# Moving four small on-chip transfers to later places in the sync queue of an attention and spectral-mix kernel

## Chip, cores and metric

The kernel runs on one core of a Trainium2 chip. The metric is device time in microseconds (us), the median of several executions. The trace has its own clock, which starts at the first instruction; its span is 1.7 to 2.6 us shorter than the measured time.

## The reference

Two steps, in float32: causal attention in a sliding window of 64 positions, then a mix in frequency space with a residual, a channel product and a rectification.

```python
x = attention(q, k, v)                      # 8 batches, 8 heads, 576 positions, 64 wide
X = np.fft.rfft(x, axis=1)                  # first 64 modes only
Yr = einsum(Xr, w_r) - einsum(Xi, w_i)      # one 512 x 512 complex matrix per mode
Yi = einsum(Xr, w_i) + einsum(Xi, w_r)
u = x + irfft(Y)                            # 8 x 576 x 512
out = u + maximum(u @ w_ch, 0)
```

## The kernel before

Most of the time goes into streaming the weights of the 64 modes. The change lies in the last 34 us, the **output stage**. By then the spectrum of each batch lies in a tile of 128 rows, of which only the last eight are missing: they belong to the last four modes, whose weights come last. One product brings these rows of all batches into one tile, `yl`. For each of batches 2 to 7, eight rows are carried from there to partitions 120 to 127 by a transfer from one on-chip tile to another, 32 KB each:

```python
def send(b):
    r0 = 2 * R + RL * (b - 2)               # RL = 8
    nc.sync.dma_start(out=batch_tile(b)[128 - RL:].bitcast(FP32), in_=yl[r0:r0 + RL].bitcast(FP32))
```

Then 36 row tiles of 128 x 512 are made. PE transforms the spectrum back (`add`), ACT rectifies, PE adds the rest, DVE adds the residual (`finish`), and the sync queue (SP) writes the result, two tiles in one transfer of 512 KB. A fifth, half-length tile of a batch pair goes out as two transfers of 64 rows.

```python
def finish(n):
    b, t = seq[n]
    add(n, "Yb", True)
    ...
    nc.vector.tensor_tensor(out=ot[:, j], in0=ps, in1=x_sb[:, b, t, :], op=ALU.add)
    if t == NT - 1:
        for i, queue in enumerate((nc.sync, nc.sync)):                  # L885
            queue.dma_start(out=out[b + i, 128 * t:, :], in_=ot[64 * i:64 * i + 64, 0])
    elif j:
        nc.sync.dma_start(out=out[b, ...], in_=ot)                      # L890, 512 KB

for n in range(NT):
    rectify(n)                                                          # add(n, "yw"), then Relu on ACT
    if n == 2:
        nc.scalar.copy(out=yl[0:NR, 0], in_=psw[0:NR])
send(2)
turn_of = {1: 3, 3: 4, 5: 5, 7: 6, 8: 7}     # after row tile n, the rows of this batch
for n in range(NQ):
    finish(n)
    if n in turn_of:
        send(turn_of[n])
    ...                                      # rectify(n + 3): up to three tiles ahead
```

So rows and outputs share one queue, which takes its instructions in order.

The softmax here doesn't subtract the row's maximum and nothing guards it: scores larger than these inputs give would overflow.

Of the kernel before, what the change touches and what calls it, by code (L numbers as in the profile page):

```python
# [20 lines left out]
def view(ap, off, dims):  # L21

    return bass.AP(ap.tensor, ap.offset + off, [list(ap.ap[0])] + [list(d) for d in dims])
# [3 lines left out]
def kernel(  # L27
# [662 lines left out]
    def batch_tile(b):  # L690

        if b not in Yp:
            Yp[b] = wmid.tile([128, 2, DM], FP32R, name=f"Y{b}", tag=f"wm{b}")
        return Yp[b]

    def pair_tile(what, b):

        return batch_tile(b)[:, ("yw", "Yb").index(what), :]

    def parts_of(b, t):  # L700
        return [(b, 0, 128)] if t < NT - 1 else [(b, 0, 64), (b + 1, 64, 64)]
# [5 lines left out]
    def turned(lhs, m, psa, psw):  # L707
        for e in range(NC):
            nc.tensor.matmul(out=psw[:m, :], lhsT=lhs(e), rhs=wch[:, e, :], start=(e == 0), stop=(e == NC - 1))  # L709
        for e in range(NC):  # L710
            nc.tensor.transpose(out=psa[:m, e, :], in_=lhs(e), identity=ident_r)
# [34 lines left out]
    def on_act(n):  # L746
        return n >= len(PLACES) and (seq[n][1] == NT - 1 or n in (11, 16, 19, 25, 30, 33))

    def lay(n):
        ps = tps[n] = bank([128, DM], FP32, "pso8")  # L750
        if on_act(n):
            nc.scalar.copy(out=ps, in_=channel_out(tiles.index(seq[n])))
            return
        nc.tensor.matmul(out=ps, lhsT=ident_r, rhs=channel_out(tiles.index(seq[n])), start=True, stop=False,
                         skip_group_check=True)
# [78 lines left out]
    with tc.manual_schedule(engines={mybir.EngineType.PE, mybir.EngineType.Activation, mybir.EngineType.DVE,  # L834
                                     mybir.EngineType.Pool, mybir.EngineType.SP}):
        nc.vector.tensor_copy(out=view(YT2, R - RL, [[NR, NC], [R, 2], [1, RL]]),
                              in_=view(psl, 0, [[RL * B, NC], [RL, 2], [1, RL]]))
        nc.vector.tensor_copy(out=YT2[:, :, 2 * R:], in_=psl[:, :, 2 * RL:])
        psa = ps_a.tile([128, NC, 128], FP32R, name="psa", tag="psa")
        psw = ps_a.tile([128, DM], FP32, name="psw", tag="psw")  # L840
        turned(lambda e: YT2[:, e, 0:NR], NR, psa, psw)
        lay(EARLY_ROWS)
        flat = psa.rearrange("p c e -> p (c e)")
        yl = yp.tile([128, 2, DM], FP32R, name="yl")

        def send(b):
            r0 = 2 * R + RL * (b - 2)
            nc.sync.dma_start(out=batch_tile(b)[128 - RL:].bitcast(FP32), in_=yl[r0:r0 + RL].bitcast(FP32))

        for b in range(2):  # L850
            nc.scalar.copy(out=pair_tile("yw", b)[E0:], in_=psw[R * b:R * b + R])
            nc.vector.tensor_copy(out=pair_tile("Yb", b)[E0:], in_=flat[R * b:R * b + R])
        nc.vector.tensor_copy(out=yl[0:NR, 1], in_=flat[0:NR])

        def add(n, what, stop):
            b, t = seq[n]
            for bb, r0, k in parts_of(b, t):
                tr = 128 * t + (64 - r0 if t == NT - 1 else 0)
                nc.tensor.matmul(out=tps[n], lhsT=trigI[:, tr:tr + 128], rhs=pair_tile(what, bb),  # L859
                                 start=False, stop=stop and r0 + k == 128, skip_group_check=True)  # L860

        def rectify(n):
            add(n, "yw", True)
            nc.scalar.activation(out=tps[n], in_=tps[n], func=ACT_F.Relu)  # L864

        ots = {}
# [4 lines that stand above are left out]
            if t % 2 == 0:  # L871
                ots[0] = op.tile([128, 2, DM], FP32, name="ot")
            ot, j = ots[0], t % 2
            ps = tps.pop(n)
            if n == NQ - 1:
                to = out[b, 128 * t - 128:128 * t + 128, :].rearrange("(p j) e -> p j e", j=2)
                for c0, queue in ((0, nc.sync), (DM // 2, nc.scalar)):
                    cc = slice(c0, c0 + DM // 2)
                    nc.vector.tensor_tensor(out=ot[:, 1, cc], in0=ps[:, cc], in1=x_sb[:, b, t, cc], op=ALU.add)
                    queue.dma_start(out=to[:, 1, cc], in_=ot[:, 1, cc])  # L880
                return
# [4 lines that stand above are left out]
            elif n == NQ - 2:  # L886
                nc.sync.dma_start(out=out[b, 128 * t:128 * t + 256, :].rearrange("(p j) e -> p j e", j=2)[:, 0],
                                  in_=ot[:, 0])
            elif j:
                nc.sync.dma_start(out=out[b, 128 * t - 128:128 * t + 128, :].rearrange("(p j) e -> p j e", j=2),  # L890
                                  in_=ot)

        AHEAD = 3
        for n in range(NT):
            rectify(n)
            if n == 2:
                nc.scalar.copy(out=yl[0:NR, 0], in_=psw[0:NR])
        send(2)
        turn_of = {1: 3, 3: 4, 5: 5, 7: 6, 8: 7}
        for n in range(NQ):  # L900
            finish(n)
            if n in turn_of:
                send(turn_of[n])
            nxt = n + AHEAD + 2
            new = nxt if n and EARLY_ROWS < nxt < NQ else None
            if new and on_act(new):
                lay(new)
            for r in {2: [5]}.get(n, [n + AHEAD] if AHEAD <= n < NQ - AHEAD else []):
                rectify(r)
            if new and not on_act(new):  # L910
                lay(new)
# [30 lines left out]
```

## Time and profile before

| | before |
|---|---|
| time, median of the first 3 runs | 429.73 us (429.59 to 430.24) |
| span of the trace | 427.3 us (its run took 429.12 us) |
| output stage, from ACT's first copy of the last rows (393.70) to the end of the span | 33.64 us |
| end of the last DVE instruction | 420.39 us |
| last packet of output ends | 426.1 us |

Three more lines of the windows view are needed for the comparison later (columns: stretch, its length, busy time and count of PE, PEld, DVE, ACT and POOL, PE clock, DMA share, GB/s).

```profile
410.00:413.00 3.00, 3.00 (x15) 2.41 (x14) 2.90 (x5) 3.00 (x7) 0.00 (x0) 1.00 0.98 358
416.00:419.00 3.00, 3.00 (x12) 1.76 (x10) 3.00 (x6) 2.55 (x6) 0.00 (x0) 1.00 1.00 370
419.00:422.00 3.00, 0.10 (x1) 0.00 (x0) 1.39 (x4) 0.00 (x0) 0.00 (x0) 1.00 1.00 372
```

The DMA share says how much of the 16 engines' time is covered by packets, GB/s how much they moved. The two must be read together: a packet that is held up counts as busy. In this trace packets of 4 KB lasted 0.159 us at the median and up to 1.03 us.

### The profile page before, as it was taken

What the parts mean: (1) busy time and instruction counts of PE and PEld (TensorE: products, weight loads), DVE (VectorE), ACT (ScalarE), POOL (GpSimd) and SP (SyncE); (2) the same over time, 40 slices, a digit from 0 to 9 for tenths busy, and PEclk for the clock granted to TensorE, in tenths of its full rate; (3) what the DMA queues carried; (4) which work ended last, traced back from release to release, by engine and by line L of the source; (5) the groups of instructions that cost most, each with busy time, mean ns of one, the idle gap of its engine ahead of it and who ended that gap; (6) DMA issues with size and microseconds to landing.
All of it is one profiled execution on the core that took longest, in us unless ns stands there. A gap on an engine that the chain in (4) does not pass through costs nothing.

```text
span 427.3 us, 11629 instructions
## 1 busy us (share of the span) xinstructions
PE 322.1 (75%) x5179; PEld 230.8 (54%) x5186; DVE 176.1 (41%) x372; ACT 164.1 (38%) x290; POOL 89.4 (21%) x171
## 2 busy tenths in 40 slices
PE   6989998998998866422488877876367685498992
PEld 5755765765665566411367666654245452266781
DVE  5566765765764200306223332221113332141993
ACT  4585765866863221001022322222012221131991
POOL 7231231241112232211221221221111122100000
PEclk9999998999996655555588998899556965589997
DMA  7999999999999999999999999999999999993698
GB/s 142 212 213 213 213 212 213 214 211 214 214 213 213 214 213 261 214 214 213 213 213 215 213 212 214 214 214 213 212 215 213 214 213 214 214 214 68 219 351 333
DMA packets 28721, 92.16 MB, mean 216 GB/s; under 512 B 2896, under 2 KB 3152, under 8 KB 28672
## 3 DMA queue, kind: packets, MB, share of 16 engines
q0 software_dynamic: 25344, 81.80, 96.1%
q1 hardware_dynamic: 3184, 9.50, 6.0%
q8 instruction: 40, 0.66, 0.6%
q10 hardware_dynamic: 144, 0.13, 0.1%
q14 instruction: 9, 0.07, 0.0%
HBM read 162.53 MB, written 9.44 MB: 402 GB/s over the span
## 4 chain that ended last, share of the span: by engine, by line
DMA 51%; PE 32%; DVE 8%; issue 4%; ACT 2%; POOL 1%; DVEq 0%; POOLq 0%
DMA wt<-in_moe_w_i_dram 45%; PE pso L316 7%; PE pst L218 6%; DMA wy<-in_moe_w_i_dram 4%; PE pso L859 4%; PE psv L235 3%; DVE x_sb L324 3%; PE pss L372 3%; PE pss L272 2%; DMA wt<-in_moe_w_r_dram 2%; PE psx L338 2%; PE pss L291 2%; DVE vT L59 2%; PE psw L709 1%; DVE ot L882 1%
## 5 line engine op out<-in xcount | busy, mean ns | idle before, releaser
L563 PE MATMUL psy<-XQ,wt 128*128 128x16 bf16 x1616 | 61.4, 191 | 72.8 <-DMA wt<-in_moe_w_i_dram 37.6
L563 PEld LDWEIGHTS <-wt 128*128 128x128 bf16 x1616 | 53.2, 103 | 87.5 <-DMA wt<-in_moe_w_i_dram 42.4
L591 DVE CAST xT<-pxt 128x256 fp32r<-128x256 bf16 (+1 forms) x68 | 26.1, 434 | 61.8 <-PE pxt L584 39.4
L115 POOL DMA_DIRECT2D wt<-in_moe_w_r_dram x54 | 29.0, 537 | 87.8 <-DMA wt<-in_moe_w_r_dram 42.2
L596 ACT CAST Z<-psz 128x512 fp32r<-128x512 f32 x36 | 21.1, 586 | 66.9 <-PE psz L594 66.6
L115 POOL DMA_DIRECT2D wt<-in_moe_w_i_dram x52 | 27.9, 536 | 84.7 <-DMA wt<-in_moe_w_i_dram 53.7
L594 PE MATMUL psz<-wch,xT 128*128 128x512 f32 x144 | 45.3, 457 | 0.0
L297 ACT ACTIVATE et<-pss 128x512 bf16<-128x512 f32 x72 | 39.2, 599 | 13.2 <-PE pss L291 13.2
L316 PE MATMUL pso<-vt,et 128*64 128x65 bf16 (+1 forms) x576 | 34.3, 210 | 5.2 <-DVE x_sb L324 5.1
L316 PEld LDWEIGHTS <-et 128*64 128x64 bf16 (+1 forms) x576 | 23.9, 114 | 17.3 <-issue 9.8
L594 PEld LDWEIGHTS psz<-wch,xT 128*128 128x128 f32 x144 | 29.2, 217 | 5.8 <-ACT Z L596 0.4
L324 DVE TENSOR_TENSOR x_sb<-pso,rcp 128x640 bf16<-128x640 f32 x32 | 26.3, 822 | 0.9
L859 PE MATMUL pso<-Y,trigI 128*128 128x512 f32 x80 | 23.1, 402 | 0.1
L59 DVE CAST YT<-psy 128x256 fp32r<-128x256 f32 x6 | 2.5, 423 | 49.4 <-PE psy L563 49.4
L882 DVE TENSOR_TENSOR ot<-pso,x_sb 128x512 f32<-128x512 f32 x35 | 22.2, 685 | 1.5 <-PE pso L859 1.1
L59 DVE CAST x_sb<-psj 128x512 bf16<-128x512 f32 x16 | 11.0, 688 | 27.2 <-PE psj L771 27.1
L58 ACT CAST YT<-psy 128x256 fp32r<-128x256 f32 x6 | 2.2, 373 | 50.7 <-DVE YT L59 50.7
L272 PE MATMUL pss<-band,ident_bf 64*64 64x512 bf16 x136 | 20.5, 414 | 1.5 <-ACT et L297 1.5
L59 DVE COPY vT<-pst 128x768 bf16<-128x768 bf16 x16 | 15.3, 957 | 13.0 <-PE pst L218 13.0
L58 ACT CAST x_sb<-psj 128x512 bf16<-128x512 f32 x16 | 9.4, 586 | 26.9 <-PE psj L771 26.9
L864 ACT ACTIVATE pso<-pso 128x512 f32<-128x512 f32 x36 | 19.1, 597 | 0.0
L859 PEld LDWEIGHTS pso<-Y,trigI 128*128 128x128 f32 x80 | 14.5, 188 | 5.5 <-ACT pso L864 1.7
(158 smaller groups left out, 496.3 us busy)
## 6 DMA issues: line engine op xcount, KB each, us to landing
wt<-in_moe_w_r_dram POOLq DMA_DIRECT2D x54, 512.0 KB, 19.1
wt<-in_moe_w_i_dram POOLq DMA_DIRECT2D x52, 512.0 KB, 19.1
out_dram<-ot SPq DMA_DIRECT2D x15, 512.0 KB, 4.2
rk<-in_k_dram POOLq DMA_DIRECT2D x8, 576.0 KB, 9.0
rq<-in_q_dram POOLq DMA_DIRECT2D x8, 576.0 KB, 12.9
rv<-in_v_dram POOLq DMA_DIRECT2D x8, 576.0 KB, 11.9
wy<-in_moe_w_r_dram POOLq DMA_DIRECT2D x3, 512.0 KB, 16.9
wy<-in_moe_w_i_dram POOLq DMA_DIRECT2D x3, 512.0 KB, 19.1
```

The costliest lines, as they stand in the source:

```text
L59: return nc.vector.tensor_copy(out=o, in_=i)
L115: nc.gpsimd.dma_start(out=wt, in_=src[m].rearrange("(p c) e -> p c e", c=NC))
L218: nc.tensor.transpose(out=ps[64 * hh:64 * hh + 64, c, :], in_=src[:, hh, (c0 + c) * D:(c0 + c + 1) * D], identity=ident_bf)
L272: nc.tensor.matmul(out=pss[(2 * w + hh) % 3][64 * half:64 * half + 64, :], lhsT=ident_bf[pp, pp], rhs=view(band[pp], 128 * half, [[0, WIN ...
L297: nc.scalar.activation(out=et[:, hh, :], in_=pss[(2 * w + hh) % 3], func=ACT_F.Exp, scale=EX_SCALE)
L316: nc.tensor.matmul(out=pso[po, hh, (i // 2) * VW:(i // 2) * VW + D + 1], lhsT=et[pk, hh, col:col + 64], rhs=vt[pk, 1 - f % 2, 2 * hh + g / ...
L324: nc.vector.tensor_tensor(out=view(x_sb, b * NT * DM + g * D, [[4 * D, 2], [DM, NT], [1, D]]), in0=view(pso, 0, [[512, 2], [VW, NT], [1, D]]),
L563: nc.tensor.matmul(out=psy[:, m % MG, e, :], lhsT=w[:, c, 128 * e:128 * e + 128], rhs=XQ[:, c, :, 1 - im:3 - im, m], start=(m % MG == im + ...
L591: nc.vector.tensor_copy(out=xT[:, :, w * k:w * k + w], in_=view(psts[k], j, [[128, NC], [n, w]]))
L594: nc.tensor.matmul(out=psz, lhsT=xT[:, c, :], rhs=wch[:, c, :], start=(c == 0), stop=(c == NC - 1))
L859: nc.tensor.matmul(out=tps[n], lhsT=trigI[:, tr:tr + 128], rhs=pair_tile(what, bb), start=False, stop=stop and r0 + k == 128, skip_group_c ...
L882: nc.vector.tensor_tensor(out=ot[:, j], in0=ps, in1=x_sb[:, b, t, :], op=ALU.add)
```

## The change

Batch 2 and batch 3 stay where they were. The rows of batches 4 to 7 move to later places, so that the first outputs are not held up behind transfers that nobody needs yet. Each still leaves eight or more tiles ahead of its first use.

```diff
-        turn_of = {1: 3, 3: 4, 5: 5, 7: 6, 8: 7}
+        turn_of = {1: 3, 5: 4, 9: 5, 12: 6, 15: 7}
         for n in range(NQ):
             finish(n)
             if n in turn_of:
                 send(turn_of[n])
```

## The prediction

> **What bounds the kernel now.** I began with the page. Its utilisation rows cut the span into 40 slices of 10.7 us.
>
> ```profile
> span 427.3 us, 11629 instructions
> ...
> PE   6989998998998866422488877876367685498992
> ...
> DMA  7999999999999999999999999999999999993698
> GB/s 142 212 213 213 213 212 213 214 211 214 214 213 213 214 213 261 214 214 213 213 213 215 213 212 214 214 214 213 212 215 213 214 213 214 214 214 68 219 351 333
> ```
>
> Up to about 391 us the DMA engines bring in weights at nines. The change touches nothing there. It acts in the last three and a half slices, where the row of DMA reads 3, 6, 9, 8: the output stage. It starts when PE begins the inverse transform at 394.3 us, and 36 row tiles pass through PE, ACT, DVE and the sync queue. So the second view is the chain of waits in order of time, and its last piece matters.
>
> ```profile
> 420.06 0.33 DVE ot L879
> ```
>
> All arithmetic is done at 420.4 us, yet the span is 427.3 us. For the last 7 us only data already computed is travelling. The chain calls the stage PE and DVE; the last instruction it can name is DVE's, so I checked the transfers myself, with the windows view (columns: busy time and count of PE, PEld, DVE, ACT, POOL, then PE clock, DMA share, GB/s).
>
> ```profile
> 399.00:401.00 2.00, 2.00 (x10) 1.60 (x9) 1.71 (x4) 2.00 (x6) 0.00 (x0) 1.00 0.98 320
> 401.00:403.00 2.00, 2.00 (x10) 1.52 (x10) 1.91 (x5) 2.00 (x6) 0.00 (x0) 1.00 0.89 340
> 403.00:405.00 2.00, 2.00 (x11) 1.61 (x10) 1.80 (x3) 2.00 (x6) 0.00 (x0) 1.00 0.94 375
> 405.00:407.50 2.50, 2.50 (x12) 2.05 (x11) 2.40 (x5) 2.50 (x6) 0.00 (x0) 1.00 0.70 216
> 407.50:410.00 2.50, 2.50 (x12) 2.01 (x11) 2.30 (x5) 2.50 (x6) 0.00 (x0) 1.00 1.01 398
> 413.00:416.00 3.00, 3.00 (x15) 2.42 (x14) 2.68 (x5) 2.98 (x7) 0.00 (x0) 1.00 1.03 407
> 422.00:425.50 3.50, 0.00 (x0) 0.00 (x0) 0.00 (x0) 0.00 (x0) 0.00 (x0) 0.50 1.01 391
> ```
>
> From 407.5 to 425.5 us the 16 DMA engines are full (share 1.0). The stage is bound by the writing of 9.4 MB of output. Before 407.5 us there is one hole: 0.70 between 405.0 and 407.5. Every microsecond lost there appears at the end, because nothing behind it has slack to recover it. The timeline of the sync queue shows who made the hole (start, length, line; L848 is the last rows' transfer, L890 an output of two tiles, L885 the two half outputs of a last row tile).
>
> ```profile
> 401.52 0.65 SPq L848 DMA_DIRECT2D Y<-yl  x1
> 402.22 0.88 SPq L890 DMA_DIRECT2D out_dram<-ot  x1
> 403.26 0.65 SPq L848 DMA_DIRECT2D Y<-yl  x1
> 404.02 1.42 SPq L885 DMA_DIRECT2D out_dram<-ot  x2
> 405.55 0.68 SPq L848 DMA_DIRECT2D Y<-yl  x1
> 406.33 0.85 SPq L890 DMA_DIRECT2D out_dram<-ot  x2
> 407.27 2.16 SPq L885 DMA_DIRECT2D out_dram<-ot  x2
> ```
>
> Between the 512 KB output issued at 402.22 and the next one at 406.33 lie 4.1 us with two small transfers of last rows and only 256 KB of output. One 512 KB output keeps the engines busy for about 1.27 us (128 packets at a median of 0.159 us, over 16 engines), the pair of L885 for about 0.7. So about 2 us of work stood against 4.1 us: the queue ran dry. DVE was not late: the tiles of the output issued at 406.33 were ready at 403.6, those of the following one at 405.1. The sync queue, issuing small transfers, was.
>
> **What the Trainium skill says.** The page "Perfetto Trace Analysis", section "What "DMA-bound" means", names as one case the DMA sequencer whose track is solid DMA slices, that time being descriptor generation. The trace agrees for 402 to 407 us only; later the engines themselves are full. The same page, section "DMA Instruction — HWDGE (DVE, Sync)", says that the profiled window of such an issue does not contain the data's movement. The trace agrees: the output issued at 397.94 first moves many packets at about 399.0, and the one at 406.33 at about 407.3, so an issue feeds the engines 1.0 us later. "DMA: Bandwidth & Descriptors", section "Why a DMA increments its semaphore by 16 and not by 1", says a transfer issued this way uses the largest number of engines up to 16 that divides its slowest dimension; eight rows therefore use 8. The trace agrees: each of these six transfers moves eight packets of 4096 bytes. The same page, section "Issuing engines are not separate DMA queues", says all issuers share the same 16 engines; so the small transfers always take some DMA time, wherever they stand.
>
> **The change part by part.** Nothing is added or removed: six transfers of 32 KB before and after, the same instructions in the same order on PE, DVE, ACT and POOL. Only SP's order differs. The rows of batch 4 leave after row tile 5 instead of 3, batch 5 after 9 instead of 5, batch 6 after 12 instead of 7, batch 7 after 15 instead of 8. Each costs the sync queue 0.65 to 0.68 us plus 0.1 for the semaphores ahead of it.
>
> I lay SP's list anew with these durations, 0.5 us for an output not held up, and no issue before DVE's result:
> - Output 5 (named by its last tile) goes at 400.2 instead of 400.85, output 7 at 401.7 (its tile is ready at 401.62) instead of 402.22.
> - The halves of tile 8 go at 402.5 and 403.2 instead of 404.02 and 404.85.
> - Batch 5's rows at 403.95; output 10 at 404.65 instead of 406.33; output 12 at 405.15 instead of 406.80.
> - Batch 6's rows at 405.7, the halves of tile 13 from 406.4 instead of 407.27, output 15 at 408.0 to 408.7 instead of 409.52, batch 7's rows next.
>
> Now the engines, 1.0 us behind. Work that arrives from 399.0: outputs 1, 3, 5, 7 are 5.1 us, tile 8 0.7, three small transfers about 0.15 to 0.4 each. The engines have work until about 405.7, and output 10 arrives at 405.7. So the 2.5 us hole closes almost wholly: (1 - 0.70) x 2.5 = 0.75 us won. From 401 to 405 the loss is 0.11 x 2 + 0.06 x 2 = 0.34 us, and I count a third of it, 0.1. Against this I leave 0.1 us for what remains at the seam. Sum: 0.75 + 0.1 - 0.1 = **0.75 us** less. After 407.5 SP has room for the two late transfers: 16.5 us pass up to its last issue, but unhindered issues there would need about 10 (seven of L890 at 0.5, six of L885 at 0.65, plus gaps, an estimate). The last results stay at 420.4 us; the last two issues are now 1.7 and 2.5 us behind DVE, so pulling them 0.75 us forward is possible.
>
> **The rivals.**
> - **The late rows make PE wait.** Batch 7 is first read by PE at 412.4 us. Its transfer now starts at 408.4 to 409.3, behind three outputs. In the kernel before these transfers landed 2.4 to 3.6 us after issue, outputs in the full stretch 3.5 to 5.0. That gives 410.8 to 412.9, at worst over 413: PE could wait up to about 1 us. For it: the queue is fuller there. Against it reaching the end: the DMA backlog is some 4 us deep then and the outputs concerned are issued 1.3 to 2.5 us after DVE. It would cost at most 0.3 us, giving 429.3.
> - **The small transfers cost more in a full queue.** Eight packets around 400.5 us took about 0.9 us each instead of 0.16, half of the engines, which is about 0.4 us of the 16; later ones took about 0.3 us per packet. If each of the three moved transfers cost 0.4, the gain would be gone: 429.9. I hold this for unlikely, since the four later ones were cheap.
> - **The hole is hidden anyway**, if PE and DVE set the end: then 429.7. Against it: 7 us of transfers after the last DVE instruction.
> - **More is won**: all of 405 to 407.5 and 401 to 405, which is 1.1 us: 428.6.
>
> **Range and chances.** 429.73 - 0.75 = 428.98, rounded to 428.95 us. Below it, the largest win and a little noise give 428.3; above it, the rival of dear transfers gives 429.9. The three runs of before spread over 0.65 us, which is nearly the effect itself. Two per cent would be 8.6 us, and the whole stage's idle DMA time is about 1.1 us: within 2% at 0.98.
>
> **What would show it.** Right: the DMA share between 405 and 407.5 rises from 0.70 to over 0.9; the second output after tile 8 is issued before 405.5 instead of 406.80; DVE still ends within 0.3 us of 420.4; the last SP issue and the span end about 0.75 us earlier. Wrong: a wait of PE's loads at L859 for the DMA of the last rows near 409 or 412 us together with a later DVE end; or an unchanged end in spite of a filled hole, with low GB/s at a share of 1.0 where the small transfers now lie, which would mean the transfers' own cost was moved and not the issue time.

## The result

| | before | changed |
|---|---|---|
| median | 429.81 us (429.59 to 430.24, 4 runs) | 429.67 us (429.39 to 430.07, 4 runs) |
| ratio | | 0.9996, 95% interval 0.9979 to 1.0014 |
| output stage in the trace | 33.64 us | 33.70 us |

Ratios are the mean time of one kernel's runs over that of the other's in the same rounds, so not quite the ratio of the medians. No difference between the two kernels can be told from the noise. A later set of five runs says the same (`after_again`: 1.0005, interval 0.9991 to 1.0018). The profiled run of the changed kernel was the slowest of its four, 430.07 us, and that of the kernel before, 429.12 us, was faster than all four of its timed runs above. The changed kernel's output stage began 0.47 us later; so I compare the stages from their own beginnings. There is only one trace of the kernel before, so how far its own stage varies is not known.

The page of the changed kernel, its span, and its rows for DMA:

```profile
span 427.9 us, 11629 instructions
...
DMA  7999999999999999999999999999999999993698
GB/s 143 212 212 213 213 214 213 213 212 212 215 212 209 214 214 259 215 213 214 213 213 214 213 214 214 213 214 214 214 213 213 213 214 214 213 213 62 228 349 325
```

Slices of 10 us show nothing: the digits are the same. The windows view, with the stretches of before moved by 0.47 us, shows more:

```profile
401.47:403.47 2.00, 2.00 (x10) 1.53 (x9) 1.91 (x5) 2.00 (x6) 0.00 (x0) 1.00 0.92 360
403.47:405.47 2.00, 2.00 (x11) 1.60 (x10) 1.80 (x3) 2.00 (x5) 0.00 (x0) 1.00 1.01 369
405.47:407.97 2.50, 2.50 (x12) 2.04 (x11) 2.40 (x5) 2.50 (x6) 0.00 (x0) 1.00 0.86 318
407.97:410.47 2.50, 2.50 (x12) 2.01 (x11) 2.29 (x5) 2.50 (x6) 0.00 (x0) 1.00 0.95 337
410.47:413.47 3.00, 2.58 (x12) 1.74 (x10) 2.90 (x5) 2.92 (x6) 0.00 (x0) 1.00 0.97 357
416.47:419.47 3.00, 3.00 (x14) 2.15 (x12) 2.99 (x6) 3.00 (x7) 0.00 (x0) 1.00 0.95 350
419.47:422.47 3.00, 0.87 (x2) 0.25 (x2) 2.17 (x5) 0.32 (x1) 0.00 (x0) 1.00 0.99 344
```

Read the last column against the lines of before. In the stretch of the hole the changed kernel moves 318 GB/s in place of 216: (318 - 216) x 2.5 us = 255 KB more. In the very next stretch it moves 337 in place of 398, (398 - 337) x 2.5 = 152 KB less. The two late stretches give back (370 - 350) x 3 = 60 and (372 - 344) x 3 = 84 KB. In these traces the gain is there, and it is handed back before the end. Summed over all packets of the output queues, rows included, from the stage's beginning, the changed kernel is ahead of the kernel before by:

| us after the stage's beginning | 13.8 | 16.3 | 19.3 | 22.3 | 25.3 | 28.3 |
|---|---|---|---|---|---|---|
| changed, KB ahead | 289 | 145 | 130 | 101 | 46 | -49 |
| changed, second trace | 297 | 140 | 92 | 49 | 31 | -79 |

At about 410 GB/s, the highest rate of a stretch, 289 KB are 0.70 us: what the prediction promised, at the place where it promised it.

Not every column can be taken as it stands. The half outputs go in packets of 2 KB, which took longer for their bytes: 0.107 us on average in the changed kernel, against 0.171 us for packets of twice the size. At 16.3 us the changed kernel has 222 of these packets behind it and the kernel before 143, so a part of the drop there is only their order. At 13.8, 19.3, 25.3 and 28.3 us the counts are equal, to two packets. Read from those columns, more than half of the lead is gone 5.5 us after the hole, and all of it at 28.3 us.

What follows the hole is in the timeline of the sync queue of the changed kernel (start, length, line):

```profile
403.16 1.82 SPq L885 DMA_DIRECT2D out_dram<-ot  x2
405.09 0.68 SPq L848 DMA_DIRECT2D Y<-yl  x1
405.87 0.85 SPq L890 DMA_DIRECT2D out_dram<-ot  x2
406.89 0.69 SPq L848 DMA_DIRECT2D Y<-yl  x1
407.67 1.83 SPq L885 DMA_DIRECT2D out_dram<-ot  x2
409.59 0.53 SPq L890 DMA_DIRECT2D out_dram<-ot  x1
410.23 0.69 SPq L848 DMA_DIRECT2D Y<-yl  x1
```

There are three of the four moved transfers (the first, of batch 4, went at 401.08), each followed by outputs that come 0.7 us later for it. And there is something else: the pair at 403.16 took 1.82 us for its two issues, where before it took 1.42. The queue is not free to issue whenever it wants.

The waits show a second cost, first the kernel before, then the changed one (waiting engine and line, what it waited for: total us, times, longest):

```profile
DVE ot L882 <- PE pso L859: 1.1, 5, 0.3
```

```profile
DVE ot L882 <- PE pso L859: 1.9, 5, 1.0
PEld pso L859 <- DMA Y<-yl: 0.9, 1, 0.9
```

PE's weight load waits 0.9 us for the rows of batch 7, which were issued at 410.23 and had landed at 413.5. DVE loses 0.8 us by it. The chain of waits ends with the same instruction as before, 0.78 us later from the stage's beginning (27.47 against 26.69 us):

```profile
421.30 0.33 DVE ot L879
```

### The profile page after: what moved, and what is told of

The parts are those of the page before. It is cut to its first block, busy times and chain, and to the rows that moved or that the text cites. A ratio compares the mean times of both kernels' runs of the same rounds, so it can differ in the third digit from the quotient of the medians.

```text
span 427.9 us, 11629 instructions
## 1 busy us (share of the span) xinstructions
PE 324.8 (76%) x5179; PEld 232.9 (54%) x5186; DVE 176.8 (41%) x372; ACT 164.1 (38%) x290; POOL 89.2 (21%) x171
## 4 chain that ended last, share of the span: by engine, by line
DMA 54%; PE 30%; DVE 8%; issue 3%; ACT 2%; POOL 1%; DVEq 0%; POOLq 0%; SPq 0%
DMA wt<-in_moe_w_i_dram 41%; DMA wy<-in_moe_w_r_dram 9%; PE pso L316 7%; PE pst L218 6%; PE psv L235 3%; DMA wt<-in_moe_w_r_dram 3%; DVE x_sb L324 3%; PE pss L372 3%; PE pso L859 2%; PE pss L272 2%; DVE ot L882 2%; PE psx L338 2%; PE pss L291 2%; DVE vT L59 2%; ACT vt L58 1%
## 5 line engine op out<-in xcount | busy, mean ns | idle before, releaser
L594 PE MATMUL psz<-wch,xT 128*128 128x512 f32 x144 | 47.6, 475 | 0.0
L594 PEld LDWEIGHTS psz<-wch,xT 128*128 128x128 f32 x144 | 30.8, 229 | 6.2 <-ACT Z L596 0.3
L58 ACT CAST x_sb<-psj 128x512 bf16<-128x512 f32 x16 | 9.4, 585 | 25.3 <-PE psj L771 25.3
```

The source lines that it names most:

```text
L594: nc.tensor.matmul(out=psz, lhsT=xT[:, c, :], rhs=wch[:, c, :], start=(c == 0), stop=(c == NC - 1))
```

## The experiments

Two theories stood at the start. **Theory A**: the gain is eaten by PE's wait for late rows. **Theory B**: the hole in the DMA's work only moved. For the second set a third was put on record, **theory C**: each small transfer holds up the eight engines that it uses, these finish every later output late, and the sync queue is held by them. That set's results suggested another form, which I use below: the small transfers take DMA time of their own, which cost nothing while it lay in the hole. In the expectations, "1.4 us" and "2.0 us" of PE's wait are the wait of the weight load and that of the matmul added up; they lie partly beside each other, so the real waits are 0.9 and 1.2 us.

For each trace I also summed the durations of all packets of the output queues, divided by 16 (**DMA work**), and took what is left between the tenth large packet and the last one (**DMA idle**). Packets overlap a little, so these sums are good to perhaps 0.2 or 0.3 us, and two traces of the same changed kernel differ by 0.57 us in the stage.

| run | median us | before | ratio (95% interval) | stage us | DMA work us | DMA idle us |
|---|---|---|---|---|---|---|
| before | | | | 33.64 | 26.00 | 0.93 |
| changed | 429.67 | 429.81 | 0.9996 (0.9979 to 1.0014) | 33.70 | 26.29 | 0.70 |
| after_again | 430.32 | 430.07 | 1.0005 (0.9991 to 1.0018) | 34.27 | 26.39 | 1.14 |
| b7_early | 429.92 | 429.58 | 0.9995 (0.9971 to 1.0019) | 33.89 | 26.25 | 0.94 |
| b7_later | 430.15 | 429.58 | 1.0003 (0.9980 to 1.0027) | 34.35 | 26.45 | 1.20 |
| pool_sends | 429.92 | 429.58 | 1.0000 (0.9975 to 1.0024) | 34.30 | 26.64 | 1.11 |
| halves | 432.82 | 429.58 | 1.0071 (1.0048 to 1.0095) | 36.81 | 26.16 | 3.71 |
| tiny_before | 429.91 | 429.81 | 0.9995 (0.9983 to 1.0007) | 33.75 | 25.12 | 1.83 |
| tiny_after | 429.26 | 429.81 | 0.9988 (0.9975 to 1.0001) | 32.90 | 25.14 | 0.94 |
| pool_rest | 429.88 | 429.81 | 1.0019 (0.9987 to 1.0052) | 32.93 | 25.98 | 0.14 |
| no_sends | 428.18 | 429.81 | 0.9969 (0.9954 to 0.9984) | 32.08 | 24.88 | 0.95 |
| copy_early | 429.85 | 430.07 | 0.9996 (0.9983 to 1.0008) | 33.57 | 26.31 | 1.01 |
| pool_paced | 429.88 | 430.07 | 0.9989 (0.9977 to 1.0002) | 33.66 | 26.67 | 0.49 |
| halves_spread | 432.56 | 429.94 | 1.0062 (1.0044 to 1.0079) | 36.67 | 26.24 | 3.29 |

### b7_early: the last two batches land in time

```diff
-        turn_of = {1: 3, 5: 4, 9: 5, 12: 6, 15: 7}     (changed kernel)
+        turn_of = {1: 3, 5: 4, 9: 5, 10: 6, 12: 7}
```

> The changed kernel, but batch 6's rows leave after row tile 10 and batch 7's after 12 (instead of 12 and 15), so that they land before PE needs them near 412.9 us. Theory A (PE's wait of 1.4 us for batch 7's rows ate the gain): the wait is gone, DVE ends about 1 us earlier than in the changed kernel, and the time is 428.9 to 429.2 us. Theory B (the sync queue's own outputs hold it up and the hole in the DMA only moved): the wait is gone too, but the time stays within 0.2 us of 429.7, and the DMA's idle time between its first and last output packet stays near 1.4 us.

PE no longer waits for rows, and DVE ends at 26.66 us of the stage, as in the kernel before. The time did not move. Theory A alone is out: the gain stays away without the wait too. The windows, aligned to the stage again, show where it goes:

```profile
405.19:407.69 2.50, 2.50 (x12) 2.04 (x11) 2.40 (x5) 2.50 (x6) 0.00 (x0) 1.00 0.86 319
407.69:410.19 2.50, 2.50 (x12) 2.02 (x11) 2.30 (x5) 2.50 (x6) 0.00 (x0) 1.00 0.84 290
```

Both late transfers now stand in the second stretch, and it falls to 290 GB/s (398 in the kernel before). The lead drops from 297 KB to 38 KB at once. The hole moved, as theory B said.

### b7_later: the last batch still later

```diff
-        turn_of = {1: 3, 5: 4, 9: 5, 12: 6, 15: 7}     (changed kernel)
+        turn_of = {1: 3, 5: 4, 9: 5, 12: 6, 18: 7}
```

> The changed kernel, but batch 7's rows leave only after row tile 18 instead of 15, so about 2 to 3 us later: PE must wait for them some 3 to 4 us instead of 1.4. Theory A (such a wait passes on to the end): 431 to 432.5 us, with a hole in the DMA after 416 us. Theory B (the backlog of the DMA, some 4 us, swallows it): at most 430.3 us.

```profile
DVE ot L882 <- PE pso L859: 4.8, 7, 2.3
ACT pso L864 <- PE pso L859: 3.1, 2, 2.0
PEld pso L859 <- DMA Y<-yl: 2.2, 1, 2.2
```

DVE ends 2.85 us later in the stage than in the changed kernel (30.32 against 27.47). The stage is 0.65 us longer than in the first trace of the changed kernel and 0.08 us longer than in the second; the time is within the noise. The backlog of the DMA swallows nearly all of a wait of this length, as theory B expected and theory A did not.

### pool_sends: the sync queue issues outputs only

```diff
-            nc.sync.dma_start(out=batch_tile(b)[128 - RL:].bitcast(FP32), in_=yl[r0:r0 + RL].bitcast(FP32))
+            nc.gpsimd.dma_start(out=batch_tile(b)[128 - RL:].bitcast(FP32), in_=yl[r0:r0 + RL].bitcast(FP32))
```

> The kernel before, with all six transfers of last rows issued by the otherwise idle POOL engine, so that the sync queue issues outputs only and all rows land by about 405 us. If the small transfers' issue time on the sync queue made the hole (Theory A, and the prediction): no wait of PE, outputs after row tile 8 issued near 404 and 405.2 us, hole closed, 428.6 to 429.0 us. Theory B (the sync queue is held up by its own outputs): the time stays within 0.3 us of 429.8, with single issues of 1 us and more already before 405 us.

The first output starts 0.8 us earlier, and still there is no gain. All six transfers now go at once, batch 2's rows come too late, and PE's load waits:

```profile
PEld pso L859 <- DMA Y<-yl: 1.2, 1, 1.2
```

In this trace the next output is issued only at 402.80 us, 2.5 us after the one before it. Later, one issue of a half output takes 1.72 us, from 414.04 on, and 0.3 to 0.6 us after its end only two to four packets are under way at a time, where 16 are usual. The landing records fit a queue that was held while engines that had run ahead ran dry: of the output issued at 412.44, 15 engines had finished within 0.55 us, one came 1.38 us after the first. That is a reading, in the sense of theory B. The single issues of 1 us and more before 405 us that theory B had named did not come; the longest took 0.85. And the run mixes two causes, so it settles less than I wanted.

### halves: twice as many small transfers, the same bytes

```diff
-            nc.sync.dma_start(out=batch_tile(b)[128 - RL:].bitcast(FP32), in_=yl[r0:r0 + RL].bitcast(FP32))
+            for i in range(2):
+                nc.sync.dma_start(out=batch_tile(b)[128 - RL:, i].bitcast(FP32),
+                                  in_=yl[r0:r0 + RL, i].bitcast(FP32))
```

> The kernel before, with each transfer of last rows cut into two of half the bytes: twelve issues instead of six, the same bytes, so 6 x 0.7 us more of the sync queue's time between 397 and 406 us. If the issue time of these transfers decides how full the DMA is (the prediction): the hole before 407.5 us grows by 2 to 3.5 us and the time is 431.5 to 433.5 us. If it is hidden behind the sync queue's other waits (Theory B): under 430.5 us.

As the prediction's mechanism said: six more issues of 0.62 to 0.68 us, and 3.2 us more at the end. DMA work stays at 26.2 us, DMA idle grows from 0.93 to 3.71. Its windows (this trace's stage begins 2.1 us later than before's):

```profile
405.00:410.00 5.00, 5.00 (x23) 4.06 (x22) 4.68 (x9) 5.00 (x12) 0.00 (x0) 1.00 0.70 250
410.00:413.00 3.00, 3.00 (x15) 2.40 (x14) 2.80 (x5) 3.00 (x8) 0.00 (x0) 1.00 0.60 163
```

So the issue time of small transfers does reach the end of the kernel. This part of the prediction's reasoning holds.

### tiny_before and tiny_after: the same issues, hardly any bytes

Both give a wrong result: each transfer carries 64 bytes of each of its eight rows. (The comparison with the reference did not flag it; it is wrong by construction all the same.) Nothing else differs from the kernel before and the changed kernel.

```diff
-            nc.sync.dma_start(out=batch_tile(b)[128 - RL:].bitcast(FP32), in_=yl[r0:r0 + RL].bitcast(FP32))
+            nc.sync.dma_start(out=batch_tile(b)[128 - RL:, 0, 0:16].bitcast(FP32),
+                              in_=yl[r0:r0 + RL, 0, 0:16].bitcast(FP32))
```

> Wrong result on purpose: the kernel before, with the six transfers of last rows in the same places, but each carrying only 64 bytes of each of its eight rows (0.5 KB instead of 32 KB). The sync queue still issues all six; the DMA engines hardly work for them. Theory of the issue time (the prediction): the hole at 405 to 407.5 us stays and the time is within 0.2 us of the kernel before, the output stage 33.4 to 33.7 us long. Theory C (each transfer holds up the eight engines it uses by 0.5 to 1 us, those eight then finish every later output late, and the sync queue is held by the slow ones): the landings of one output stay within 0.5 us of each other, and the time is 0.5 to 1 us below the kernel before.

> Wrong result on purpose: the changed kernel, with its transfers of last rows in their later places but carrying only 64 bytes per row. Against the run with small transfers in the old places this shows what the new places are worth when the transfers cost no DMA time. Theory of the issue time: 0.7 to 0.9 us below the kernel before, since the hole closes and the rows land soon enough that PE waits little. Theory C: at least as far below the kernel before as the other one, 1 to 1.5 us, with no split of landings in two halves of eight after 411 us.

The stretch of the hole in the old places, then in the new ones (the stages of both traces begin at 393.73 us, as good as in the kernel before):

```profile
405.00:407.50 2.50, 2.50 (x12) 2.04 (x11) 2.40 (x5) 2.50 (x7) 0.00 (x0) 1.00 0.76 230
```

```profile
405.00:407.50 2.50, 2.50 (x12) 2.02 (x11) 2.39 (x5) 2.50 (x7) 0.00 (x0) 1.00 0.88 347
```

With the issues kept and the bytes gone, the time did not fall by the 0.5 to 1 us that theory C had named for `tiny_before`. The four kernels make a square:

| stage us / DMA work / DMA idle | old places | new places |
|---|---|---|
| 32 KB | 33.64 / 26.00 / 0.93 | 33.70 / 26.29 / 0.70 (second trace 34.27 / 26.39 / 1.14) |
| 0.5 KB | 33.75 / 25.12 / 1.83 | 32.90 / 25.14 / 0.94 |

Go down the left column: the bytes are taken away, the DMA has 0.88 us less to do, and the stage is not shorter; the idle time grows by 0.90 instead. This says that in the old places the transfers' DMA time lay in the hole and was free. Go along the lower row: with no bytes, the new places shorten the stage by 0.85 us, what the prediction gave for the change. Go along the upper row: with the bytes, nothing. In the new places they add 1.15 to 1.25 us of DMA work (26.29 and 26.39 less 25.14), and PE has to wait for them. In `tiny_after` PE does not wait for rows.

The lead, counted as above, divides the loss in two. `tiny_after` is ahead of `tiny_before` by 411 KB at 13.8 us, 222 at 19.3 and 244 at 28.3, three points at which both have sent equally many packets of half outputs. So up to 19.3 us about as much of the lead is lost without the bytes (189 KB) as with them (289 less 130, 159 KB): there the hole has moved, as theory B said. After 19.3 us the lead stays without the bytes; with them it falls from 130 to -49 KB, and in the second trace from 92 to -79. PE's wait for batch 7's rows falls in that time too; `b7_early`, which has the bytes but not the wait, loses its lead sooner (33 KB at 19.3 us) and then little more (-15 at 28.3).

The times agree in direction: medians of 429.91 and 429.26, spans of 426.6 and 427.2 to 427.8 us against 426.6 to 427.0. But their intervals overlap; the square rests on the traces. Three of its cells have one trace each, and the two traces of the fourth differ by 0.57 us where the square's effect is 0.85. It is evidence, not proof.

The landing records show how a transfer of eight rows does more than take its own time. Sorted landing times of the 16 engines for the first output issued after batch 7's rows, in us after the first engine:

```
changed     0.00 0.02 0.05 0.09 0.12 0.14 0.15 0.17 | 0.38 0.41 0.56 0.59 0.66 0.76 0.91 1.07
tiny_after  0.00 0.11 0.16 0.17 0.19 0.20 0.21 0.27 | 0.28 0.30 0.31 0.32 0.34 0.37 0.39 0.48
```

Eight engines are on time, eight are behind. Only eight packets carried the rows. The next output is split the same way, the two after it less cleanly. The queue's next issues are among the longest of the stage (1.24, 1.16 and 1.45 us), and near 416.7 us only 7 packets are under way. That the slow eight hold the queue up is my reading of this; no run tried it alone, and some of the records speak against it: in the second trace the split is there too, but at least 12 packets are under way all through that stretch, and `tiny_before`, with hardly any bytes, has issues of 1.27 and 1.52 us.

### no_sends: the ceiling

```diff
-            nc.sync.dma_start(out=batch_tile(b)[128 - RL:].bitcast(FP32), in_=yl[r0:r0 + RL].bitcast(FP32))
+            return
```

> Wrong result on purpose: the kernel before without any of the six transfers (the last eight rows of six batches keep zeros that were written earlier). The ceiling of what any placing of them can win. If issue time and DMA time of the transfers are what the stage loses: the output stage of the trace shrinks from 33.6 us to 31.5 to 32.5 us, time 427.6 to 428.6 us. If something else binds (the rate of the output's own packets, or PE and DVE): at most 0.5 us below the kernel before.

Wrong: the rows keep zeros. The stage is 1.56 us shorter and the median 1.6 us lower. About 0.8 us of this is the first output's earlier start, since batch 2's rows no longer stand ahead of it. I take it as the ceiling of what a placing of the six transfers can win.

### pool_rest, copy_early and pool_paced: attempts at a faster version

`pool_rest` keeps batch 2 on the sync queue and gives the other five to POOL at once.

```diff
+            queue = nc.sync if b == 2 else nc.gpsimd
-            nc.sync.dma_start(out=batch_tile(b)[128 - RL:].bitcast(FP32), in_=yl[r0:r0 + RL].bitcast(FP32))
+            queue.dma_start(out=batch_tile(b)[128 - RL:].bitcast(FP32), in_=yl[r0:r0 + RL].bitcast(FP32))
```

> A right result: the kernel before, but only batch 2's rows leave from the sync queue (first in it, while the DMA engines are empty), those of batches 3 to 7 from the idle POOL engine at once. In the run with all six on POOL, PE waited 2.0 us for batch 2's rows; this takes that wait away. Theory of the issue time: hole closed, no wait of PE, 0.7 to 1.1 us below the kernel before. Theory C: five transfers still hold up engines, now all near 400 us, and outputs land split; at most 0.4 us below it.

Median 429.88 against 429.81 us, ratio 1.0019 (0.9987 to 1.0052). Its spans run from 427.1 to 432.5 us, and the trace is of the shortest; I build nothing on that trace. It is no faster.

`copy_early` is the changed kernel with batch 2's rows ready one ACT instruction sooner.

```diff
-            if n == 2:
+            if n == 1:
                 nc.scalar.copy(out=yl[0:NR, 0], in_=psw[0:NR])
```

> A right result: the changed kernel, with ACT's copy of the last rows moved ahead of the third rectification, so that batch 2's rows can leave about 0.6 us earlier, while the DMA engines are still empty, and the first output is not held up behind them. If the DMA engines bound the stage, their start 0.5 us earlier is a gain of 0.3 to 0.6 us against the changed kernel: stage 33.1 to 33.4 us. If ACT, PE or DVE bind it, no gain.

The DMA starts 0.5 us sooner in the stage (4.99 against 5.48 us), the stage is 33.57 us: 0.13 us less than one trace of the changed kernel and 0.70 less than the other, and above the 33.1 to 33.4 that I had expected. The time is not told apart from the kernel before.

`pool_paced` adds to this that batches 3 to 7 leave from POOL, each held back by a tiny copy of the tile just finished.

```diff
+            queue = nc.sync if b == 2 else nc.gpsimd
...
-        turn_of = {1: 3, 5: 4, 9: 5, 12: 6, 15: 7}
+        turn_of = {1: 3, 4: 4, 7: 5, 10: 6, 12: 7}
             if n in turn_of:
+                nc.gpsimd.tensor_copy(out=gate, in_=ots[0][0:1, seq[n][1] % 2, 0:1])
                 send(turn_of[n])
```

> A right result: as the run before it, and in addition batches 3 to 7 leave from POOL, each held back by a tiny copy that waits for row tile 1, 4, 7, 10 or 12. It takes the issue time off the sync queue and keeps the transfers apart, but not their DMA time. Expected: no PE wait over 0.5 us, no hole at 405 to 407.5 us, stage 32.3 to 32.9 us (the run without any transfers had 32.08, the transfers' DMA time is about 0.8), time 0.7 to 1.3 us below the kernel before. If the DMA time of the transfers and the split of the engines cost more than that: no faster than the run before it.

PE does not wait, DMA idle falls to 0.49 us, the lowest of all but the untrusted trace of `pool_rest`. And DMA work rises to 26.67 us. The stage is 33.66 us, not the 32.3 to 32.9 I had expected, and the ratio 0.9989 (0.9977 to 1.0002) leaves open whether there is a gain at all. No version beats both kernels clearly.

### after_again: the changed kernel once more

> The changed kernel once more, unaltered, for a second trace and a closer ratio. So far: the new places win 0.85 us of the stage when the transfers carry almost nothing (33.75 to 32.90 us) and nothing when they carry their 32 KB (33.64 to 33.70). Expected: the stage 33.5 to 33.9 us, the time within 0.3 us of the kernel before, PE again waiting about 1 to 1.5 us for batch 7's rows, and outputs after that transfer landing in two groups of eight engines.

The time is as expected; the stage of 34.27 us is outside my range of 33.5 to 33.9, with a wait of 1.2 us for batch 7's rows. It shows how far two traces of one kernel lie apart, and it repeats the rise and fall of the lead in the table above.

### halves_spread: the doubled transfers in the new places

```diff
-        turn_of = {1: 3, 3: 4, 5: 5, 7: 6, 8: 7}       (halves)
+        turn_of = {1: 3, 5: 4, 9: 5, 12: 6, 15: 7}
```

> The run with twelve half transfers, now in the changed kernel's later places. There the hole made by issue time is far larger than in the real kernel (DMA idle 3.7 us of the stage against 0.9), while the bytes are the same. If spreading works by taking issue time out of the early stretch, and fails in the real kernel only because the transfers' DMA time, hidden in the hole before, then has to be paid, it must win here: four issues of 0.7 us leave the early stretch, 1 to 2 us less than the 432.8 us of the run in the old places, so 430.8 to 431.8 us. If issue time on the sync queue does not matter to the end, or PE's wait for the later rows takes it all: 432.4 us or more.

This run is a miss. The win is 0.3 us of the medians, ratios 1.0062 against 1.0071 with overlapping intervals. DMA idle falls only from 3.71 to 3.29 us, since each pair of issues makes a new hole behind its new place. Two of its stretches:

```profile
407.50:409.00 1.50, 1.50 (x8) 1.17 (x7) 1.50 (x4) 1.50 (x4) 0.00 (x0) 1.00 0.44 157
411.00:412.00 1.00, 1.00 (x6) 0.82 (x5) 0.90 (x2) 1.00 (x3) 0.00 (x0) 1.00 0.61 152
```

The pairs were issued at 406.3 and 408.9 us. Besides, batch 7's rows came so late that PE's load waited 2.7 us and DVE 5.1 us in all. So this run cannot serve as proof that spreading wins once the hole is large; it shows that issue time costs in the new places as well.

## Why the prediction was right or wrong

The measured 429.67 us is inside the range of 428.3 to 429.9 us, and "within 2%" was right. That says little: the range reached up far enough to hold the kernel before itself, 429.73 us, and so no change at all. The point, 0.75 us of gain, was not confirmed: the medians differ by 0.14 us in one set and by -0.25 in the other, and both intervals contain no change.

- **What bounds the stage** was right. Doubling the issues cost 3.2 us with DMA work unchanged; taking the transfers away won 1.6 us.
- **The hole and its cause** were right, and so was its size: 0.70 us of lead at 13.8 us of the stage, against 0.75 predicted. The DMA share of the stretch rose to 0.86, short of the 0.9 that I had asked for.
- **The order of issues** was too hopeful. I took 0.5 us for an output "not held up"; output 7 took 1.01 us and the second half of tile 8 took 1.22. So outputs 10 and 12 went at 405.4 and 405.9 us (with the stage's shift taken off) and not at 404.65 and 405.15. The sign I had set, before 405.5 us, was missed.
- **The step that failed** is "After 407.5 SP has room for the two late transfers". Its sum took every issue as unhindered, 0.5 us for one of L890 and 0.65 for one of L885, and counted seven of L890 where the trace has nine. In the kernel before these issues took 0.68 and 1.12 us on average, and with the last two 15.2 us of the 16.5: the queue was as solid with issues there as between 402 and 407 us, which the prediction had denied. The DMA was not free either: `b7_early`, with both late transfers in the stretch after the hole, moved 290 GB/s there where the kernel before moved 398.
- **The rival that small transfers cost more in a full queue** was called unlikely, and is a part of the answer, though not as worded. Its 0.4 us for each of the moved transfers was too much: all six took 1.15 to 1.25 us of DMA work in the new places and 0.88 in the old. What the square points to is that this time was free only while the hole was there. The rival would have made it 429.9; it came to 429.67.
- **The rival that PE waits for late rows** was right in size: 0.9 and 1.2 us in two traces against "up to about 1 us". By itself it costs little, as `b7_later` shows.
- **The rival that the hole is hidden** by PE or DVE was wrong: DVE's end moved by 2.85 us in `b7_later` and the time hardly did.

What stays open, beyond that rough division at 19.3 us: how much of the lead is lost to the transfers' own packets, how much to their issue time and how much to the split of the engines. Their sum is what the traces show, their shares are not.

## What to carry to other kernels

When two things share a full resource, a hole in its use is not all gain: see first what else lies in the hole for free, because filling it sends the bill for that. Follow the bytes moved since the beginning of the stage, aligned to that beginning, and not only the hole; that shows at once whether a lead is kept. And test a suspected transfer with its issue kept and its bytes taken away, in both orders: four runs help to tell issue time, transfer time and their interplay apart, if each has more than one trace.

## What the Trainium skill lacked or had wrong

- "Perfetto Trace Analysis", section "DMA Instruction — HWDGE (DVE, Sync)", says what the issue's window contains, not how much it varies. In the kernel before, the same output of 512 KB took 0.37 to 1.17 us to issue, the 64-row half 0.59 to 1.31 us.
- "DMA: Bandwidth & Descriptors", section "Why a DMA increments its semaphore by 16 and not by 1", tells which engines a transfer of eight rows uses. It lacks what can follow for others: in the changed kernel the output issued after batch 7's rows landed in two groups of eight engines, up to 0.17 us and 0.38 to 1.07 us after the first.
- The same page, section "Issuing engines are not separate DMA queues", calls the issue time saved "usually small relative to the DMA itself". Here it was not small: six transfers of 32 KB took 4.1 us to issue (0.65 to 0.78 each) for about 0.9 us of DMA work, and six more such issues cost 3.2 us. Giving the six to another engine won nothing all the same (`pool_sends`, ratio 1.0000).
- No page that I read gives the duration of a 4 KB packet between two on-chip tiles: in `pool_sends`, where these packets have a queue of their own, 0.159 to 1.18 us with a median of 0.185. The median of the output's packets of this size is 0.159.
